# Scaling the values instead of the keys, and a last output tile in two halves, in a linear-attention and gated-MLP kernel

## The chip, the cores and the metric

The kernel runs on one core of one Trainium2 chip. The metric is the device time of one execution in microseconds (us), as a median over several runs. The core has five engines that work side by side and meet only at semaphores: TensorE (matmuls, PE in the profile), VectorE (DVE), ScalarE (ACT), GpSimd (POOL) and SyncE (SP, which here only starts transfers). TensorE writes to PSUM, eight banks of 512 fp32 columns; VectorE and ScalarE read PSUM[...].

## The reference

A token row of 2048 x 512 is layer-normalized, and two branches of it are added to the input: a linear attention with 32 heads of 16, and a gated MLP.

```python
qkv = (x @ wqkv) ...                      # q, k, v: (B, H, S, 16)
pq = einsum("bhsd,hdf->bhsf", q, w_phi)
pk = einsum("bhsd,hdf->bhsf", k, w_phi)
phi_q = concat([softmax(pq), softmax(-pq)])      # 32 features a head
phi_k = concat([softmax(pk), softmax(-pk)])
kv = einsum("bhsf,bhsd->bhfd", phi_k, v)
z  = einsum("bhsf->bhf", phi_k)
o  = einsum("bhqf,bhfd->bhqd", phi_q, kv) / (einsum("bhqf,bhf->bhq", phi_q, z) + 1e-6)
A  = o.reshape(B, S, D) @ wo
B  = (gelu(xn @ w_gate) * (xn @ w_up)) @ w_down  # 1376 wide
out = x + A + B                                  # xn = layernorm(x)
```

What matters for the change: a softmax over the 16 features of one head and one sign divides by a sum per token, head and sign. In the sum over tokens that makes `kv` and `z`, this divisor may be put on the key's exponentials or on the value and on a 1 beside it; the product is the same.

## The kernel before

The program lists its operations with what they read and write, and a small scheduler on the host puts them in an order for each engine; that order is fixed when the kernel runs. `BK` are the eight PSUM banks. The work goes by 16 tiles of 128 tokens. It starts with normalization, the first quarter of the MLP and the folding of `w_phi` into the key and query weights. Then comes the key/value stage (some 31 to 80 us of the span), and then attention output, the rest of the MLP and the output products, interleaved.

Start, with TensorE's spare matmuls, whose results nobody reads:

```python
op("pe", [... e.matmul(bank(7), warm[:, 0:128], warm[:]) for _ in range(11)], ...)
for t in range(4):
    ln_stats(t, ...); ln_rstd(t, 1); ln_norm(t)
    xt_pe(t, 4 + t % 2)            # 4 transposes on TensorE, copied to xnT by ScalarE
    if t < 2:
        op("pe", [... e.matmul(bank(3), warm[:, 0:128], warm[:]) for _ in range(2)], ...)
for t in range(4):
    gate4(t)                       # 16 matmuls of 128 columns
```

Key/value stage, by tile:

```python
def proj_k(t, b):                  # bank b from a ring of 4, shared with proj_q
    # 4 matmuls of 512 columns, then on ScalarE exp(+s) and exp(-s):
    e.activation(Ek[:, t, :, sig, :], bank(b)..., ACTF.Exp, scale=(1.0, -1.0)[sig])
    if t in SDVE:                  # (3, 7, 11, 15): one tensor_reduce on VectorE
        ...
    # the other 12 tiles: four halving additions on GpSimd, 512, 256, 128, 64 elements
    op("pool", ... e.tensor_tensor(o, a[:, :, 0:n], a[:, :, n:2 * n], op=ALU.add), ...)

def k_norm(t):                     # VectorE
    op("dve", ... e.reciprocal(rk[:, k, :], Ssum[:, t, :]), ...)
    op("dve", ... e.tensor_tensor(ev, ev, r, op=ALU.mult), ...)       # 1024 bf16, in place

def v_out(t, b):                   # copies V out of PSUM, ScalarE or VectorE
    alt([("act", ... ACTF.Copy), ("dve", ... tensor_copy)], ...)

def kv_acc(t):                     # banks 6 and 7, summed over all tiles
    for i in range(8):             # 4 heads x both signs on one side, 4 x 16 values and a 1
        e.matmul(ps[:, 3072 + i * 128:3072 + i * 128 + VB], Ek[:, t, i, :, :], vs[:, k, i, :], ...)
                                   # VB = 65 columns
def kv_finish():                   # 8 masked copies of 64 partitions into kvr
    ...
```

The output product of a tile, and what ends the kernel for the last four:

```python
def outp(t, b, direct):
    # 4 matmuls with wo and 11 with w_down, 512 columns each, into bank b
    if direct:
        op("dve", ... e.tensor_tensor(ob[:, k, :], bank(b), x_all[:, t, :], op=ALU.add), ...)
    ...
    dma("sp", ... e.dma_start(out2[t * P:(t + 1) * P, :], ob[:, k, :]), ...)
while outs < NT:
    outp(outs, (7, 0, 1, 2)[outs - 12], True)
```

Of the kernel before, what the change touches and what calls it, by code (L numbers as in the profile page):

```python
# [9 lines left out]
P = 128  # L10
# [10 lines left out]
VB = 4 * DH + 1  # L21
# [178 lines left out]
def bass_parallel_sum__linear_kernel_hedgehog__glu_gated_geglu__prompt_kernel(  # L200
# [14 lines left out]
    with ExitStack() as es, nc.allow_low_precision("bf16 softmax factors"):  # L215
# [13 lines left out]
        mask4 = sb([P, 4], f32, "mask4")  # L229
        hmask = sb([P, 8], f32, "hmask")  # L230
# [28 lines left out]
        NVS = 8  # L259
        vs = sb([P, NVS, 8, VB], bf16, "vs")  # L260
        NRK = 2
        rk = sb([P, NRK, 64], bf16, "rk")

# [15 lines left out]
        with nc.sbuf_tensor("Ek", [P, NT, 8, 2, 64], bf16) as Ek:  # L279
            pass  # L280
# [53 lines left out]
        B_rk = bufs("rk", NRK)  # L334
        B_vs = bufs("vs", NVS)
        B_m4, B_hm, B_v1 = Buf("m4"), Buf("hm"), Buf("v1")
        B_Eq = [bufs(f"Eq{s}_", 8) for s in range(NST)]
        B_wqT = B_Eq[3][0:4]
        B_kvr = bufs("kvr", 8)
# [105 lines left out]
        def proj_k(t, b):  # L445
            op("pe", [lambda e, i=i: e.matmul(  # L446
                bank(b), xnT[:, i, t * P:(t + 1) * P], wk2[:, i, :], start=(i == 0), stop=(i == 3))
                for i in range(4)], reads=[B_xnT[t]] + B_wk2, writes=[BK[b]], cost=mm(4))
            for sig in range(2):
                exps.append(op("act", lambda e, sig=sig: e.activation(  # L450
                    Ek[:, t, :, sig, :], bank(b).rearrange("p (b c) -> p b c", c=64), ACTF.Exp, scale=(1.0, -1.0)[sig]),
                    reads=[BK[b]], writes=[B_Ek[t][sig]], cost=0.55, extra=gelus, tab="exp"))
            ev = Ek[:, t, :, :, :].rearrange("p b s c -> p (b s) c")
            if t in SDVE:
                op("dve", lambda e: e.tensor_reduce(
                    Ssum[:, t, :].rearrange("p (g h) -> p g h", h=4), ev.rearrange("p g (f h) -> p g h f", h=4),
                    axis=mybir.AxisListType.X, op=ALU.add), reads=B_Ek[t], writes=[B_S[t]], cost=1.24)
                return
            v1 = st1[:].rearrange("p (g c) -> p g c", c=32)
            v2 = st2[:].rearrange("p (g c) -> p g c", c=16)  # L460
            v3 = st3[:].rearrange("p (g c) -> p g c", c=8)
            v4 = Ssum[:, t, :].rearrange("p (g c) -> p g c", c=4)
            for k, (o, a, n, bo, ba, c) in enumerate((
                    (v1, ev, 32, [B_st[0]], B_Ek[t], 1.17), (v2, v1, 16, [B_st[1]], [B_st[0]], 0.73),
                    (v3, v2, 8, [B_st[2]], [B_st[1]], 0.4), (v4, v3, 4, [B_S[t]], [B_st[2]], 0.29))):
                op("pool", lambda e, o=o, a=a, n=n: e.tensor_tensor(o, a[:, :, 0:n], a[:, :, n:2 * n], op=ALU.add),  # L466
                   reads=ba, writes=bo, cost=c, lock=k < 3)

        def k_norm(t):
            k = t % NRK  # L470
            op("dve", lambda e: e.reciprocal(rk[:, k, :], Ssum[:, t, :]), reads=[B_S[t]], writes=[B_rk[k]], cost=0.57)
            ev = Ek[:, t, :, :, :].rearrange("p b s (f h) -> p (b s) f h", h=4)
            r = rk[:, k, :].rearrange("p (g h) -> p g h", h=4).unsqueeze(2).to_broadcast([P, 16, DH, 4])
            op("dve", lambda e: e.tensor_tensor(ev, ev, r, op=ALU.mult), reads=[B_rk[k]], writes=B_Ek[t], cost=0.72,  # L474
               lock=True)
# [17 lines left out]
        def v_out(t, b):  # L493
            k = t % NVS
            dst, src = vs[:, k, :, 0:64], bank(b).rearrange("p (b c) -> p b c", c=64)
            alt([("act", lambda e: e.activation(dst, src, ACTF.Copy), 0.58),
                 ("dve", lambda e: e.tensor_copy(dst, src), 0.69)], reads=[BK[b]], writes=[B_vs[k]])

        SDVE = (3, 7, 11, 15)
        kv_first = [True, True]  # L500

        def kv_acc(t):
            k = t % NVS
            fns = []
            for i in range(8):
                st = kv_first[i // 4]
                kv_first[i // 4] = False
                fns.append(lambda e, i=i, st=st: e.matmul(  # L508
                    ps[:, 3072 + i * 128:3072 + i * 128 + VB], Ek[:, t, i, :, :], vs[:, k, i, :],
                    start=st, stop=(t == NT - 1), skip_group_check=True))  # L510
            op("pe", fns, reads=B_Ek[t] + [B_vs[k], B_v1], writes=BK[6:8], cost=8 * 0.045)

        def kv_finish():

            kv = ps[:, 3072:4096].rearrange("p (i c) -> p i c", c=128)
            for sg in range(2):
                for b2 in range(2):
                    src = kv[sg * 64:sg * 64 + 64, b2::2, :]
                    dst = kvr[b2 * 64:b2 * 64 + 64, sg * 4:sg * 4 + 4, b2 * 4:b2 * 4 + 4, :]
                    m = mask4[sg * 64:sg * 64 + 64, :].unsqueeze(1)  # L520
                    op("dve", lambda e, src=src, dst=dst, m=m: e.tensor_tensor(
                        dst[:, :, :, 0:DH], src[:, :, 0:64].rearrange("p i (h d) -> p i h d", d=DH),
                        m.unsqueeze(3).to_broadcast([64, 4, 4, DH]), op=ALU.mult),
                       reads=BK[6:8] + [B_m4, B_kvrm], writes=[B_kvr[sg * 4 + b2 * 2]], cost=dve(256))
                    op("dve", lambda e, src=src, dst=dst, m=m: e.tensor_tensor(
                        dst[:, :, :, DH], src[:, :, 64].unsqueeze(2).to_broadcast([64, 4, 4]),
                        m.to_broadcast([64, 4, 4]), op=ALU.mult),
                       reads=BK[6:8] + [B_m4, B_kvrm], writes=[B_kvr[sg * 4 + b2 * 2 + 1]], cost=0.2)
# [45 lines left out]
        def att(t):  # L574
            s, tl = t // 4, t % 4
            k = t % NB
            for q in range(3):
# [5 lines left out]
                   reads=B_Eq[s][3 * q:min(3 * q + 3, 8)] + B_kvr + [B_kvrm], writes=[BK[4 + q]],  # L583
# [61 lines left out]

        def wtrans(w, Bw, jj, b):
# [18 lines left out]
        NVG = 0  # L665
# [3 lines left out]
        for t in range(4):  # L669
# [4 lines left out]
            if t < 2:  # L674
                op("pe", [lambda e: e.matmul(bank(3), warm[:, 0:128], warm[:], start=True, stop=True)  # L675
                          for _ in range(2)], reads=[B_warm], writes=[BK[3]], cost=0.5,
                   extra=[d_tr[t]])
# [4 lines left out]
        def kq():  # L682
            turn[0] += 1
            return (turn[0] - 1) % 4
# [23 lines left out]
        for b2 in range(2):  # L708
            op("pool", lambda e, b2=b2: e.tensor_tensor(
                bd[:, :, b2 * 64:b2 * 64 + 64].rearrange("p j (f h) -> p j f h", h=4),  # L710
                mask8[:, b2 * 4:b2 * 4 + 4].unsqueeze(1).unsqueeze(1).to_broadcast([P, 4, DH, 4]),
                wphi[:].unsqueeze(3).to_broadcast([P, 4, DH, 4]),
                op=ALU.mult), reads=[B_mask8, B_wphi], writes=[B_bd], cost=0.6, lock=True,
                extra=[B_xn[3].last_write])
        op("dve", lambda e: e.tensor_reduce(
            mask4[:], idt_f[:].rearrange("p (a h) -> p h a", h=4), axis=mybir.AxisListType.X, op=ALU.add),
            reads=[B_idf], writes=[B_m4], cost=0.3)
        op("pool", [lambda e: e.memset(kvr[:].rearrange("p i h c -> p (i h c)"), 0.0),
                    lambda e: e.memset(hmask[:], 0.0)], writes=[B_kvrm, B_hm], cost=1.2)
        op("pool", lambda e: e.memset(vs[:, :, :, 64], 1.0), writes=[B_v1], cost=0.3)  # L720
        op("dve", [lambda e, b2=b2: e.tensor_copy(
            hmask[b2 * 64:b2 * 64 + 64, b2 * 4:b2 * 4 + 4], mask4[b2 * 64:b2 * 64 + 64, :]) for b2 in range(2)],
            reads=[B_m4], writes=[B_hm], cost=0.2)
        op("dve", lambda e: e.tensor_copy(
            kvr[:, :, :, VW], hmask[:].unsqueeze(1).to_broadcast([P, 8, 8])),
            reads=[B_hm], writes=[B_kvrm], cost=0.2)
# [6 lines left out]
        for jf in range(4, NF):  # L733
# [9 lines left out]
            if jf >= 6 and jf - 6 < NVG:  # L743
                proj_v(jf - 6, 4 + jf % 2)
                v_out(jf - 6, 4 + jf % 2)
# [10 lines left out]
        nk = 0  # L756

        def val(t):
            b = 4 + t % 2
            proj_v(t, b)  # L760
            v_out(t, b)

        def key():
            nonlocal nk
            k_norm(nk)
            if nk > 0:
                kv_acc(nk - 1)
            nk += 1
# [3 lines left out]
        for r in range(NT):  # L772
# [3 lines left out]
            if r + KA >= LAG:  # L776
                if NVG <= nk < NT:
                    val(nk)
                if nk < NT:
                    key()  # L780
        while nk < NT:
            if nk >= NVG:
                val(nk)
            key()
# [17 lines left out]
        while outs < NT:  # L802
            outp(outs, (7, 0, 1, 2)[outs - 12], True)
            outs += 1

# [52 lines left out]
```

## Time and profile before

| | |
|---|---|
| device time, median of 3 (lowest, highest) | 198.93 us (198.83, 199.02) |
| span of the profiled execution | 197.2 us |
| DMA | 14.41 MB, 73 GB/s on average |
| longest group of GpSimd's waits | 51.6 us, 16 times, for VectorE's `otmp` |
| longest group of ScalarE's waits | 42.1 us, 12 times, for the output products |
| final store: 16 of 128 KB, from issue to landing | 1.7 us (median) |

The profile is one execution on the chip. It has the busy time of each engine, the span in forty slices with a digit for the busy tenths, groups of instructions by source line with busy time and mean duration, waits with what ended them, and the chain of work that ended last: from the last instruction back, at each step to what released it or to the instruction before it on its engine. An engine with much idle time costs nothing as long as it doesn't keep that chain waiting. A row's mean duration of matmuls includes their overlap; what one adds to TensorE's list is read from the chain.

### The profile page before, as it was taken

How to read it: one execution, taken by the hardware profiler on the slowest of the kernel's cores; microseconds unless marked ns; L12 is line 12 of the kernel's file. 1: busy time of each engine (PE TensorE's matmuls, PEld its weight loads, DVE VectorE, ACT ScalarE, POOL GpSimd, SP SyncE). 2: the span in 40 equal slices, each digit the busy share in tenths (PEclk: the TensorE clock that was granted, in tenths of full speed). 3: DMA queues.
4: the chain of work that ended last, by engine and by line, in shares of the span. 5: the costliest groups of instructions: out<-in, count | busy, mean ns of one | idle time of the engine just before them, and what ended most of it. 6: DMA issues, size and time to landing. Idle time of an engine off the chain costs nothing.

```text
span 197.2 us, 3160 instructions
## 1 busy us (share of the span) xinstructions
PE 192.7 (98%) x1183; PEld 97.9 (50%) x1183; DVE 133.3 (68%) x312; ACT 86.2 (44%) x149; POOL 83.5 (42%) x109
## 2 busy tenths in 40 slices
PE   7999999999999999999999999999999999999994
PEld 2574665445545454554445555554545555454441
DVE  4789895469597767898695797948358494853121
ACT  2382798998887979323122132222223222221000
POOL 7731202799999996022244334242232324223100
PEclk9999999999999999999999999999999999999999
DMA  5999944456000000001221202120201111021101
GB/s 172 329 376 349 203 85 53 81 177 216 4 0 0 3 0 0 0 3 27 53 55 30 51 30 52 50 33 27 53 17 39 27 51 31 27 57 27 53 27 55
DMA packets 24079, 14.41 MB, mean 73 GB/s; under 512 B 15888, under 2 KB 23584, under 8 KB 24064
## 3 DMA queue, kind: packets, MB, share of 16 engines
q1 hardware_dynamic: 22944, 11.74, 23.4%
q0 software_dynamic: 560, 1.95, 3.1%
q10 hardware_dynamic: 560, 0.52, 0.8%
q8 instruction: 9, 0.15, 0.3%
q14 instruction: 6, 0.05, 0.1%
HBM read 8.44 MB, written 2.10 MB: 53 GB/s over the span
## 4 chain that ended last, share of the span: by engine, by line
PE 94%; DVE 2%; DMA 1%; POOL 1%; issue 0%
PE ps_all L546 35%; PE ps_all L630 18%; PE ps_all L489 7%; PE ps_all L478 7%; PE ps_all L446 7%; PE ps_all L626 7%; PE ps_all L578 4%; PE ps_all L667 2%; PE ps_all L508 2%; PE ps_all L561 2%; DMA oT<-o_sb 1%; PE ps_all L647 1%; PE ps_all L658 1%; PE ps_all L438 1%; PE ps_all L675 1%; POOL o_sb L618 1%
## 5 line engine op out<-in xcount | busy, mean ns | idle before, releaser
L546 PE MATMUL ps_all<-xnT,wu_sb 128*128 128x512 bf16 (+1 forms) x176 | 44.7, 379 | 0.0
L537 ACT ACTIVATE gs<-ps_all 128x512 bf16<-128x512 f32 (+1 forms) x44 | 25.9, 598 | 38.2 <-PE ps_all L546 38.1
L546 PE MATMUL ps_all<-xnT,wg_sb 128*128 128x512 bf16 (+1 forms) x160 | 40.9, 379 | 0.0
L630 PE MATMUL ps_all<-wd_sb,hT 128*128 128x512 bf16 (+1 forms) x176 | 40.6, 379 | 0.0
L618 POOL TENSOR_TENSOR o_sb<-otmp 128x512 bf16<-128x512 bf16 x16 | 18.5, 1154 | 51.6 <-DVE otmp L612 51.6
L539 DVE TENSOR_TENSOR hT<-gs,ps_all 128x512 bf16<-128x512 bf16 (+1 forms) x44 | 28.9, 680 | 14.7 <-PE ps_all L546 14.2
L630 PEld LDWEIGHTS ps_all<-wd_sb,hT 128*128 128x128 bf16 (+1 forms) x176 | 17.2, 98 | 20.8
L546 PEld LDWEIGHTS ps_all<-xnT,wu_sb 128*128 128x128 bf16 (+1 forms) x176 | 17.4, 100 | 19.4
L640 ACT ACTIVATE y_sb<-ps_all 128x512 f32<-128x512 f32 x12 | 7.2, 597 | 42.1 <-PE ps_all L630 42.1
L642 POOL TENSOR_TENSOR ob<-y_sb,x_all 128x512 bf16<-128x512 f32 x12 | 13.9, 1155 | 22.0 <-ACT y_sb L640 22.0
L612 DVE TENSOR_TENSOR otmp<-ps_all,cf 128x384 bf16<-128x384 f32 (+1 forms) x48 | 21.7, 507 | 0.6
L546 PEld LDWEIGHTS ps_all<-xnT,wg_sb 128*128 128x128 bf16 (+1 forms) x160 | 15.1, 100 | 13.7
L466 POOL TENSOR_TENSOR st<-st 128x256 f32<-128x256 f32 (+1 forms) x24 | 19.1, 795 | 1.8
L450 ACT ACTIVATE Ek<-ps_all 128x512 bf16<-128x512 f32 x32 | 17.3, 619 | 3.3 <-PE ps_all L446 2.9
L484 ACT ACTIVATE EqT<-ps_all 128x512 bf16<-128x512 f32 x32 | 17.8, 626 | 2.0 <-PE ps_all L478 1.7
L595 DVE RECIPROCAL r_sb<-ps_all 128x48 f32<-128x48 f32 (+1 forms) x32 | 9.2, 327 | 12.9 <-PE ps_all L578 12.8
L626 PE MATMUL ps_all<-wo_sb,oT 128*128 128x512 bf16 x64 | 16.4, 379 | 0.2 <-DMA oT<-o_sb 0.2
L489 PE MATMUL ps_all<-wv_sb,xnT 128*128 128x512 bf16 x64 | 16.4, 379 | 0.0
L478 PE MATMUL ps_all<-xnT,wq 128*128 128x512 bf16 x64 | 16.4, 379 | 0.0
L446 PE MATMUL ps_all<-wk,xnT 128*128 128x512 bf16 x64 | 15.9, 379 | 0.0
L466 POOL TENSOR_TENSOR st<-Ek 128x512 f32<-128x512 bf16 x12 | 13.9, 1157 | 3.7 <-ACT Ek L450 3.7
L474 DVE TENSOR_TENSOR Ek<-Ek,rk 128x1024 bf16<-128x1024 bf16 x16 | 14.6, 910 | 0.6
(71 smaller groups left out, 191.0 us busy)
## 6 DMA issues: line engine op xcount, KB each, us to landing
out_dram<-ob SPq DMA_DIRECT2D x16, 128.0 KB, 1.7
x_all<-in_A_x_dram SPq DMA_DIRECT2D x3, 512.0 KB, 9.3
wd_sb<-in_B_w_down_dram POOLq DMA_DIRECT2D x1, 1280.0 KB, 9.4
wg_sb<-in_B_w_gate_dram SPq DMA_DIRECT2D x2, 432.0 KB, 7.0
wu_sb<-in_B_w_up_dram SPq DMA_DIRECT2D x2, 432.0 KB, 8.1
wu_sb<-in_B_w_up_dram SPq DMA_DIRECT2D x2, 256.0 KB, 4.9
hT<-in_A_wqkv_dram SPq DMA_DIRECT2D x2, 256.0 KB, 8.0
EqT<-in_A_wqkv_dram SPq DMA_DIRECT2D x2, 256.0 KB, 9.1
```

Of the source, the lines that this page charges most:

```text
L446: op("pe", [lambda e, i=i: e.matmul(bank(b), xnT[:, i, t * P:(t + 1) * P], wk2[:, i, :], start=(i == 0), stop=(i == 3)) for i in range(4)] ...
L466: op("pool", lambda e, o=o, a=a, n=n: e.tensor_tensor(o, a[:, :, 0:n], a[:, :, n:2 * n], op=ALU.add), reads=ba, writes=bo, cost=c, lock=k < 3)
L478: op("pe", [lambda e, i=i: e.matmul(bank(b), wq2[:, i, p * 128:(p + 1) * 128], xnT[:, i, s * 512:(s + 1) * 512], start=(i == 0), stop=(i = ...
L484: exps.append(op("act", lambda e, g=g, sig=sig: e.activation(EqT[:, g, s * 512:(s + 1) * 512], bank(b), ACTF.Exp, scale=(1.0, -1.0)[sig]), ...
L489: op("pe", [lambda e, i=i: e.matmul(bank(b), xnT[:, i, t * P:(t + 1) * P], wv_sb[:, i, :], start=(i == 0), stop=(i == 3)) for i in range(4 ...
L537: h = op("act", lambda e: e.activation(gs[0:w, k, :], bank(gb)[0:w, :], ACTF.Gelu_apprx_tanh), reads=[BK[gb]], writes=[B_gs[k]], cost=0.55 ...
L539: op("dve", lambda e: e.tensor_tensor(hT[0:w, s % 2, jf, :], gs[0:w, k, :], bank(ub)[0:w, :], op=ALU.mult), reads=[B_gs[k], BK[ub]], write ...
L546: op("pe", [lambda e, i=i: e.matmul(bank(b)[0:w, :], wt[:, i, jf * 128:jf * 128 + w], xnT[:, i, s * 512:(s + 1) * 512], start=(i == 0), st ...
L612: op("dve", lambda e, q=q, n=n: e.tensor_tensor(otmp[:, k, q * 384:q * 384 + n * 128].rearrange("p (s h d) -> p s h d", s=n, d=DH), bank(4 ...
L618: op("pool", lambda e: e.tensor_tensor(o_sb[:, k, :], otmp[:, k, 0:512], otmp[:, k, 512:1024], op=ALU.add), reads=B_ot[k], writes=[B_o[k]] ...
L626: fns = [lambda e, j=j: e.matmul(bank(b), oT[:, t % NOT, j, :], wo_sb[:, j, :], start=(j == 0), stop=False) for j in range(4)]
L630: fns.append(lambda e, jf=jf, w=w: e.matmul(bank(b), hT[0:w, s % 2, jf, tl * 128:(tl + 1) * 128], wd_sb[0:w, jf, :], start=False, stop=(jf ...
```

## The change

Two things are asked of it. The normalization is moved from the exponentials of the keys to the values: the reciprocals are written beside the values as a 17th column of each head, and V is multiplied by them on its way out of PSUM. That does away with the in-place multiply of 1024 key elements and with a separate copy of V. The exponentials are kept in head order, with eight heads of one sign to a stationary tile, so each product has 8 x 17 = 136 columns, of which the blocks on the diagonal are used. The sums take three banks, so keys and queries share three in turn and values use banks 3 and 4. And the last output tile is computed in two halves of 256 columns in two banks, so that the first half's addition and store run under the second half's matmuls. The pair of spare matmuls behind the second tile's transposes goes.

```diff
-VB = 4 * DH + 1
+GV = 8 * VW                       # VW = 17
...
-        NVS = 8
-        vs = sb([P, NVS, 8, VB], bf16, "vs")
+        NVS = 5
+        vs = sb([P, NVS, 2, 4 * GV], bf16, "vs")
...
-                    Ek[:, t, :, sig, :], bank(b).rearrange("p (b c) -> p b c", c=64), ACTF.Exp, ...
+                    Ek[:, t, sig, :], bank(b), ACTF.Exp, ...
...
+            v1 = st1[:].rearrange("p (h f) -> p h f", f=8)
+            op("pool", lambda e: e.tensor_tensor(v1, ev[:, :, 0:8], ev[:, :, 8:16], op=ALU.add), ...
+            # then 4 + 4, 2 + 2 and 1 + 1 of each head
...
-        def k_norm(t): ...
-        def v_out(t, b): ...
+        def v_post(t, b):
+            op("dve", lambda e: e.reciprocal(
+                v[:, :, :, DH], Ssum[:, t, :].rearrange("p (s h) -> p s h", s=2)), ...
+            op("dve", lambda e: e.tensor_tensor(
+                v[:, :, :, 0:DH],
+                bank(b).rearrange("p (h d) -> p h d", d=DH).unsqueeze(1).to_broadcast([P, 2, 32, DH]),
+                v[:, :, :, DH].unsqueeze(3).to_broadcast([P, 2, 32, DH]), op=ALU.mult), ...
...
-                    ps[:, 3072 + i * 128:3072 + i * 128 + VB], Ek[:, t, i, :, :], vs[:, k, i, :],
+                    bank(5 + i // 3)[:, (i % 3) * GV:(i % 3 + 1) * GV],
+                    Ek[:, t, sig, p * 128:(p + 1) * 128],
+                    vs[:, k, sig, p * GV:(p + 1) * GV],
...
         def kv_finish():
-            # 8 masked copies, 64 partitions each
+            for q in range(3):     # 3 masked copies, one a bank
...
-            if t < 2:
+            if t < 1:
                 op("pe", [lambda e: e.matmul(bank(3), warm[:, 0:128], warm[:], ...) for _ in range(2)], ...
...
-            return (turn[0] - 1) % 4
+            return (turn[0] - 1) % 3
...
-            b = 4 + t % 2
+            b = 3 + nv % 2
...
-        while outs < NT:
-            outp(outs, (7, 0, 1, 2)[outs - 12], True)
+        while outs < NT - 1:
+            outp(outs, (7, 0, 1)[outs - 12], True)
             outs += 1
+        outp_halves(NT - 1, (2, 3))
```

The program's order of values, keys and products on TensorE's list changes with it: in the new one two tiles of values follow the first three of keys, and from the third tile on each tile's key-value products stand behind its own value product or the next one's.

## The prediction

> **What bounds the kernel now.** I read the page first (busy times and the forty slices), then TensorE's waits, then the chain of work that ended last in order of time, and last the rows and the timelines of the stage that the change rewrites.
>
> The page and the answer on TensorE's waits (us in total, times, longest):
>
> ```profile
> PE 192.7 (98%) x1183; PEld 97.9 (50%) x1183; DVE 133.3 (68%) x312; ACT 86.2 (44%) x149; POOL 83.5 (42%) x109
> ...
> PE   7999999999999999999999999999999999999994
> ...
> PE ps_all L667 <- DVE warm L393: 1.2, 1, 1.2
> PE ps_all L626 <- DMA oT<-o_sb: 0.2, 1, 0.2
> ```
>
> TensorE is busy in every slice but the first and the last, and after its first instruction it waits once, for 0.2 us. A busy row alone would not prove a bound, since matmuls overlap in it, so the proof is the chain (start, length, what):
>
> ```profile
> 7.85 0.22 PE ps_all L438 x4
> 8.07 0.43 PE ps_all L675 x2
> 8.51 0.67 PE ps_all L561 x12
> ...
> 40.05 0.26 PE ps_all L508 x8
> 40.31 0.86 PE ps_all L478 x4
> ...
> 83.90 0.50 PE ps_all L578 x8
> ...
> 191.87 2.39 PE ps_all L630 x11
> 194.26 0.02 issue
> 194.28 0.69 DVE ob L636
> ```
>
> The chain is 94% TensorE and its pieces join end to start. So whatever lengthens TensorE's list lengthens the kernel, and what the other engines save is worth nothing unless they come late. The chain also gives clean costs per matmul, which the mean of 379 ns in the rows does not (it contains the overlap): 0.86/4 = 216 ns at 512 columns, 0.50/8 = 62.5 ns at 144, 0.67/12 = 55.8 ns at 128, 0.26/8 = 32.5 ns at 65.
>
> The rows of VectorE that the change touches or that have a like form (busy us, mean ns):
>
> ```profile
> L612 DVE TENSOR_TENSOR otmp<-ps_all,cf 128x384 bf16<-128x384 f32 x32 | 16.4, 552 | 0.6
> L474 DVE TENSOR_TENSOR Ek<-Ek,rk 128x1024 bf16<-128x1024 bf16 x16 | 14.6, 910 | 0.6
> L612 DVE TENSOR_TENSOR otmp<-ps_all,cf 128x256 bf16<-128x256 f32 x16 | 6.6, 415 | 0.0
> ```
>
> GpSimd's timeline at the start of the same stage, tiles 0 to 2:
>
> ```profile
> 34.79 1.16 POOL L466 TENSOR_TENSOR st<-Ek 128x512 f32<-128x512 bf16 x1 [3.69 <-ACT Ek L450]
> ...
> 37.38 0.32 POOL L466 TENSOR_TENSOR Ssum<-st 128x64 f32<-128x64 f32 x1
> ...
> 44.66 1.60 POOL L466 TENSOR_TENSOR st<-st 128x256 f32<-128x256 f32 x2
> ```
>
> Tile 0's sums run from the first line shown to the second and tile 1's start at 37.66, so one tile takes GpSimd 2.87 us when left alone (its two middle sums 1.27). The last line is tile 2's middle pair, 1.60. In between stand three loads that GpSimd issues (39.40 to 41.78); they make the sums of tiles 1 and 2 the latest things in the stage.
>
> **What the Trainium skill says.** "TensorE: Matmul & The Clock Gate", section "Back-to-back issue gap": a warm matmul takes its columns over 2.4 GHz plus 2.5 ns. The trace agrees at 512, 144 and 128 columns; at 65 the formula gives 29.6 ns and the trace 32.5. The page's sustained figures with weight loads (81 ns at 128) don't hold here: 55.8 was measured with a load before each. "SBUF — State Buffer", section "Who interferes with whom": a VectorE instruction with two SBUF inputs shuts out a GpSimd instruction that reads SBUF, for its whole length. The trace agrees: the multiply of the keys takes 0.69 us alone and 1.04 otherwise, and GpSimd's pair of middle sums 1.27 us alone and 1.60 or 2.09 beside it. "VectorE: DVE Perf Modes", section "Why PSUM operands drop a tier": an fp32 operand in PSUM means the slowest mode. Row L612 agrees, at (552-415)/128 = 1.07 ns an element.
>
> **The change part by part.**
>
> *Key-value products.* Before, each of 16 tiles has 8 matmuls of 65 columns (four heads and a column of ones); after, 8 of 136 (eight heads, each with its reciprocal as a 17th column). The stationary side stays 128 wide, so nothing is won back. Between 55.8 ns at 128 and 62.5 at 144 lies 59.1 at 136: 0.473 us a tile against 0.26. 16 x 0.213 = **+3.4 us**, all on the chain.
>
> *Where the normalization sits.* Out go 16 multiplies of keys (910 ns) and the copies of V out of PSUM (9 on ScalarE of 0.61, 7 on VectorE of 0.69). In come 16 multiplies of 1024 elements out of PSUM: 552 + 640 x 1.07 = 1.24 us. VectorE pays 16 x 0.33 us more and saves 4.8: nearly even. ScalarE loses 5.5 us, GpSimd is no longer shut out. None of this lies on the chain: **0**, if nobody becomes late.
>
> *The spare matmuls.* The pair at 8.07 goes: 0.43 us. Behind it the 12 gate products of tile 0 are ready, and then come 4 of tile 1, whose copy by ScalarE ends at 8.71; TensorE would be there at 8.74. The later inputs (normalized tile 3 at 9.45, up weights issued at 3.5 to 4.4 and landing in about 5) are ready too: **-0.4 us**.
>
> *The last tile.* 30 matmuls of 256 columns, about 109 ns each, for 15 of 216: +0.03 us. The add behind the last matmul shrinks from 0.69 to about 0.42 us (the 415 of row L612 at 256 columns). The store is 64 KB where each one before is 128 KB and lands after 1.7 us, most of which I take for fixed; I allow 0.1. **-0.35 us.**
>
> *The one wait.* TensorE's 0.2 us before the third output tile: in the new order its attention products end 8.05 us before they are needed, against 7.55 before: **-0.2 us.**
>
> *New waits in the rewritten stage.* With 0.4 us gained, the first key products start at 31.0, exponentials at 33.2, GpSimd at 34.35. The sums of tile 1 are ready at about 43.0 (the three loads stand in between), its values at 44.85, TensorE reaches it at 45.3. The sums of tile 2 follow at 45.9, reciprocal and multiply by 47.7; TensorE is there at 47.5. So it waits about **+0.25 us**. Afterwards TensorE needs 3 x 0.86 + 0.47 = 3.06 us a tile, GpSimd 2.87 for three tiles of four, VectorE 0.55 for the reciprocal, 1.24, and a quarter of a 1.21 us sum, 2.1 in all, ScalarE four exponentials of about 0.5 = 2.0. All are faster than TensorE, so the lag does not come back.
>
> Sum: 3.4 - 0.4 - 0.35 - 0.2 + 0.25 = **+2.7 us**, and 198.93 + 2.7 = **201.6 us**, 1.4% more.
>
> **The rivals.**
>
> *The ring of score banks is too short.* Keys and queries get three PSUM banks in turn instead of four, values keep two, the sums take three. If ScalarE frees a bank only after TensorE wants it, TensorE waits at each group. For it: at the start ScalarE works off a backlog at 0.95 us a group against TensorE's 0.86. Against it: value and sum matmuls lie between; going through the first ten groups I find each bank free 0.5 to 1 us ahead. If it bites, about 0.2 us a tile: up to 3 us more, about 204.
>
> *VectorE or GpSimd becomes the bound.* If the new layout's short runs (8, 4, 2 and 1 elements) slow GpSimd's sums by a third, it needs 3.8 us a summed tile, 2.9 on average over four, still under 3.06, but the early wait grows to some 1 to 2 us: 202.5 to 203.5. Against it: three of its four steps read as many elements as before from tightly packed buffers.
>
> *The waits removed were worth more.* GpSimd freed from the lock and ScalarE from copies could only help if TensorE waited for them. Its waits above are 0.2 us in all, so I give this no weight. Were the wider matmuls hidden, the result would be 198.2; nothing in the chain speaks for hiding.
>
> **Range and chances.** The 3.4 us are the firm part, good to 0.2. The tail and the start may each miss by 0.2, the new waits lie between 0 and 2 us, so the range leans upwards: 200.8 to 203.0. 2% slower means 202.9, which takes one of the rivals: 0.13. Within 2%: 0.86. Faster by 2% would need 4 us from an engine that does not hold up the chain: 0.01.
>
> **What would show it.** The key-value row at 16 x 8 matmuls with about 0.47 us a tile in the chain, against 0.26; gate products straight behind the second tile's transposes; TensorE's waits a few tenths of a us, on VectorE at the third tile's sums; the last add near 0.42 us; GpSimd's middle sums at 1.27 us throughout. I am wrong if TensorE's list shows repeated waits on ScalarE (the ring) or on VectorE (late values), or if matmuls of 136 columns cost other than 59 ns.

## The result, and the profile after

| | before | after |
|---|---|---|
| device time, median of 4 runs each, side by side (lowest, highest) | 198.98 us (198.83, 199.62) | 201.30 us (200.82, 201.75) |
| ratio, 95% interval | | 1.011 [1.0076, 1.0144] |
| span of the profiled execution | 197.2 us | 199.1 us |

The changed kernel is 2.3 us slower, 1.1%. The prediction was 201.6 us, in a range of 200.8 to 203.0.

The page of the kernel after, busy times and the forty slices:

```profile
PE 195.0 (98%) x1196; PEld 102.6 (52%) x1196; DVE 130.9 (66%) x298; ACT 81.4 (41%) x140; POOL 75.6 (38%) x105
...
PE   7999999999999999999999999999999999999994
```

VectorE, ScalarE and GpSimd are less busy than before by 2.4, 4.8 and 7.9 us. TensorE is busier by 2.3 us. TensorE's waits after the change (us in total, times, longest) hold nothing from the rewritten stage:

```profile
PE ps_all L677 <- DVE warm L388: 1.2, 1, 1.2
PE ps_all L551 <- ACT xnT L437: 0.3, 1, 0.3
```

Both lie at the start. The 0.2 us for `oT<-o_sb`, the wait before the third output tile, is gone. The chain of work that ended last (start, length, what) is again TensorE's list, piece on piece:

```profile
6.91 0.38 PE ps_all L551 x4
7.29 0.22 PE ps_all L433 x4
7.51 0.67 PE ps_all L551 x12
8.18 0.02 issue
8.20 0.40 PE ps_all L551 x4
...
47.10 0.47 PE ps_all L503 x8
...
102.79 0.86 PE ps_all L616 x4
...
196.56 0.42 DVE ob L651
```

Set beside the chain before: the eight key-value products of a tile take 0.47 us where they took 0.26. The 12 gate products follow the second tile's transposes at once, but the next four take 0.40 us and not 0.22. The output tile at 102.79 starts with no gap. The last addition takes 0.42 us and not 0.69. VectorE's two new rows, as groups (busy us, mean ns, idle before and what ended it):

```profile
L487 DVE TENSOR_TENSOR vs<-ps_all,vs 128x1024 bf16<-128x1024 f32 x16 | 19.4, 1217 | 3.3 <-PE ps_all L477 3.2
L651 DVE TENSOR_TENSOR ob<-ps_all,x_all 128x256 bf16<-128x256 f32 x2 | 0.9, 426 | 2.2 <-PE ps_all L646 2.2
```

The multiply on the values takes 1.22 us, near the 1.24 worked out from a row of before. GpSimd's second sum of a tile, kept apart by shape:

```profile
L458 POOL TENSOR_TENSOR st<-st 128x256 f32<-128x256 f32 x12 | 8.8, 730 | 0.9
```

With the third, 400 ns in the same view, the middle pair takes 1.13 us in every tile, or 1.21 with the gap between the two, where 1.27 was predicted. Before, the two rows of these shapes were:

```profile
L466 POOL TENSOR_TENSOR st<-st 128x256 f32<-128x256 f32 x12 | 12.1, 1010 | 0.9
L466 POOL TENSOR_TENSOR st<-st 128x128 f32<-128x128 f32 x12 | 7.0, 580 | 0.9
```

With the pieces of the two chains the difference of the spans can be put together:

| part | from the chains | us |
|---|---|---|
| first gate product | 7.47 to 6.91 | -0.56 |
| spare pair: first gate product to first up product | 4.83 to 4.59 | -0.24 |
| key-value products, 16 tiles | 4.14 to 7.57 | +3.43 |
| wait before the third output tile | see experiments | -0.40 |
| matmuls of the last tile | 3.26 to 3.30 | +0.04 |
| end of the last matmul to the end | 2.94 to 2.57 | -0.37 |
| sum | spans: 197.2 to 199.1 | +1.90 |

Without the first row, which concerns matter ahead of everything changed, the sum is +2.46 us.

### The profile page after: what moved, and what is told of

The parts are those of the page before. It is cut to its first block, busy times and chain, and to the rows that moved or that the text cites. A ratio compares the mean times of both kernels' runs of the same rounds, so it can differ in the third digit from the quotient of the medians.

```text
span 199.1 us, 3159 instructions
## 1 busy us (share of the span) xinstructions
PE 195.0 (98%) x1196; PEld 102.6 (52%) x1196; DVE 130.9 (66%) x298; ACT 81.4 (41%) x140; POOL 75.6 (38%) x105
## 4 chain that ended last, share of the span: by engine, by line
PE 98%; DVE 0%; ACT 0%; issue 0%
PE ps_all L536 36%; PE ps_all L620 18%; PE ps_all L477 7%; PE ps_all L441 7%; PE ps_all L466 7%; PE ps_all L616 7%; PE ps_all L568 4%; PE ps_all L503 4%; PE ps_all L677 2%; PE ps_all L551 2%; PE ps_all L646 1%; PE ps_all L658 1%; PE ps_all L669 1%; PE ps_all L433 0%; PE ps_all L641 0%; ACT xnT L437 0%
## 5 line engine op out<-in xcount | busy, mean ns | idle before, releaser
L529 DVE TENSOR_TENSOR hT<-gs,ps_all 128x512 bf16<-128x512 bf16 (+1 forms) x44 | 28.7, 680 | 14.7 <-PE ps_all L536 14.6
L620 PE MATMUL ps_all<-wd_sb,hT 128*128 128x512 bf16 (+1 forms) x165 | 38.1, 379 | 0.0
L620 PEld LDWEIGHTS ps_all<-wd_sb,hT 128*128 128x128 bf16 (+1 forms) x165 | 16.1, 98 | 19.5
L487 DVE TENSOR_TENSOR vs<-ps_all,vs 128x1024 bf16<-128x1024 f32 x16 | 19.4, 1217 | 3.3 <-PE ps_all L477 3.2
L484 DVE RECIPROCAL vs<-Ssum 128x64 bf16<-128x64 f32 x16 | 8.7, 554 | 12.4 <-POOL Ssum L462 12.3
L616 PE MATMUL ps_all<-wo_sb,oT 128*128 128x512 bf16 x60 | 15.4, 379 | 0.0
```

The source lines that it names most:

```text
L487: op("dve", lambda e: e.tensor_tensor(v[:, :, :, 0:DH], bank(b).rearrange("p (h d) -> p h d", d=DH).unsqueeze(1).to_broadcast([P, 2, 32, DH]),
L529: op("dve", lambda e: e.tensor_tensor(hT[0:w, s % 2, jf, :], gs[0:w, k, :], bank(ub)[0:w, :], op=ALU.mult), reads=[B_gs[k], BK[ub]], write ...
L616: fns = [lambda e, j=j: e.matmul(bank(b), oT[:, t % NOT, j, :], wo_sb[:, j, :], start=(j == 0), stop=False) for j in range(4)]
L620: fns.append(lambda e, jf=jf, w=w: e.matmul(bank(b), hT[0:w, s % 2, jf, tl * 128:(tl + 1) * 128], wd_sb[0:w, jf, :], start=False, stop=(jf ...
```

## The experiments

Two theories were put against each other at the start. The one of the prediction: the extra columns of the key-value products are paid in full, because TensorE's list is the kernel; everything else is a few tenths. The rival: the size agrees by chance, and a good part of the loss comes from the ring of three banks, or from late values. The single parts were then measured one by one, most of them on the kernel before. A time "against before" is against runs of the kernel before on the same chip.

**One half of the change: the last tile in halves (e1_tail).** The kernel before, with the spare pair and normalized keys kept.

```diff
-        while outs < NT:
-            outp(outs, (7, 0, 1, 2)[outs - 12], True)
+        while outs < NT - 1:
+            outp(outs, (7, 0, 1)[outs - 12], True)
             outs += 1
+        outp_halves(NT - 1, (2, 3))
```

> The kernel before with only the last output tile in two halves. Theory (the tail is a serial chain behind the last matmul): matmuls of the last tile 3.30 us instead of 3.26, add behind the last matmul 0.43 instead of 0.69, end of the span 2.57 us after the last matmul instead of 2.94; in all 0.33 us less, 198.65. Rival (a store costs the same at any size): only the add shrinks, 0.22 us less. If the halves cost TensorE more than columns, the last tile takes over 3.4 us and nothing is gained.

Measured: 198.50 us (22 runs) against 198.86, ratio 0.9986 [0.9977, 0.9994], so -0.28 us by the ratio, with an interval of -0.46 to -0.12 (the medians differ by 0.36). The predicted -0.35 lies in it. Where it comes from is seen at the end of the kernel: the last addition 0.42 us in place of 0.69, and a store that lands earlier. The transfers at the end of the kernel after (KB each, median us from issue to landing):

```profile
out_dram<-ob SPq DMA_DIRECT2D x2, 64.0 KB, 1.5
```

In this view a store of half the bytes lands 0.2 us sooner after its issue than the 1.7 of the 128 KB stores. At the end of the span 0.1 us of that is left: the end follows the last matmul by 2.57 us and not 2.94, and 0.27 of these 0.37 us are the addition.

**One part: the second spare pair out (e2_nospare).** The kernel before with one edit:

```diff
-            if t < 2:
+            if t < 1:
                 op("pe", [lambda e: e.matmul(bank(3), warm[:, 0:128], warm[:], start=True, stop=True)
```

> The kernel before with only the second spare pair of matmuls taken out. Theory now: of its 0.43 us, 0.18 covered the wait for ScalarE's copy of the second tile, which then shows up in front of that tile's first gate products (0.40 us for the first four instead of 0.22); gain 0.24 us, 198.75. Rival (the prediction): gain 0.40. From the first gate product to the first 512-column product of the up weights: 4.83 us before, 4.59 by the theory, 4.43 by the rival.

Measured: 198.74 us (14 runs) against 198.86, ratio 0.9996 [0.9984, 1.0007], that is -0.32 to +0.14 us. The predicted -0.4 is outside, the -0.24 expected here inside; the time alone does not tell -0.24 from nothing. The chain does. With the pair (e1_tail):

```profile
8.13 0.22 PE ps_all L438 x4
8.36 0.43 PE ps_all L696 x2
8.79 0.67 PE ps_all L561 x12
9.46 0.22 PE ps_all L438 x4
```

Without it (e2_nospare):

```profile
8.26 0.22 PE ps_all L438 x4
8.49 0.67 PE ps_all L561 x12
...
9.18 0.40 PE ps_all L561 x4
9.57 0.22 PE ps_all L438 x4
```

From one group of transposes (L438) to the next there are 1.33 us with the pair and 1.31 us without. Removing 0.43 us of spare work wins nothing in that stretch, since the gate products of the second tile are now at the head of TensorE's list before ScalarE's copy is there. What is won comes later: those four products are then done, where with the pair they are among the 36 gate products that end the row (2.01 us; without it 32, 1.79 us). From the first gate product to the end of the last of them it is 4.84 us with the pair (7.75 to 12.59) and 4.60 without (7.88 to 12.48): -0.24 us, as in the changed kernel.

**The other half alone: the values scaled (e3_values).** The changed kernel with the old last tile and both spare pairs.

```diff
-            if t < 1:
+            if t < 2:
...
-        while outs < NT - 1:
-            outp(outs, (7, 0, 1)[outs - 12], True)
+        while outs < NT:
+            outp(outs, (7, 0, 1, 2)[outs - 12], True)
             outs += 1
-        outp_halves(NT - 1, (2, 3))
```

> The changed kernel with the old last tile and the spare pair back, so the move from keys to values alone. Theory (columns on TensorE's list): 16 x (0.473 - 0.26) = 3.4 us more, and about 0.4 less for the wait before the third output tile that the new order avoids: 3.0 us above before, 202.0. Rival (late engines, ring of three banks): TensorE's list of waits would show waits on ScalarE or VectorE between 31 and 84 us, and the sum would lie above 203.

Measured: 201.84 us (4 runs) against 198.86, ratio 1.0146 [1.0126, 1.0166], +2.9 us. TensorE has no wait in the stage, and every piece of key-value products is 0.47 us. The three parts, -0.28, -0.08 and +2.9, add up to +2.5 us; the whole change measured +2.3.

**The suspected cost taken away: products of 65 columns in the new form (e4_narrow).** The changed kernel, with its key-value products cut to the width they had before. This leaves out the products of about half of the heads.

```diff
-                    bank(5 + i // 3)[:, (i % 3) * GV:(i % 3 + 1) * GV],
+                    bank(5 + i // 3)[:, (i % 3) * GV:(i % 3) * GV + 65],
                     Ek[:, t, sig, p * 128:(p + 1) * 128],
-                    vs[:, k, sig, p * GV:(p + 1) * GV],
+                    vs[:, k, sig, p * GV:p * GV + 65],
```

> The changed kernel with its key-value products cut from 136 to 65 columns; it leaves out the products of the columns beyond, so half of the heads' sums are missing, and keeps everything else with the same order on TensorE. Theory (the columns are the whole price): 0.26 us a tile again, 3.4 us less than the changed kernel, 197.9, which is below before. Rival (layout, banks or VectorE cost something too): it stays above 199.5, with waits of TensorE in the stage.

Measured: 198.37 us (20 runs) against 198.86, ratio 0.9971 [0.9962, 0.9981]. So 201.3 falls to 198.4: 2.9 of the 3.4 us come back with the columns alone, ring, order, banks and engines being those of the change. From the first gate product to the end of the last matmul it takes 186.59 us (7.81 to 194.40), where the changed kernel has 189.62: 3.03 us less. A tile's products that wait for nothing take 0.24 us (0.26 in the kernel before), others more; the rest of the 3.43 us, 0.40, has become new waits, and with them the 197.9 us expected here were missed by 0.5. Two pieces of the chain, the first behind a wait, and TensorE's weight loads, which show on whom it waits (us in total, times, longest):

```profile
62.28 0.42 PE ps_all L503 x8
...
65.28 0.24 PE ps_all L503 x8
...
PEld ps_all L503 <- DVE vs L487: 2.2, 5, 0.6
```

With narrow products TensorE needs 2.82 us a tile (3 x 0.86 + 0.24), the kernel after's GpSimd 2.78 (36.77 - 33.99, between two tiles' first sums), and the values come late behind GpSimd's loads and behind tiles that VectorE sums. With wide products TensorE has 3.05 and the values are early. The new form would thus not have got the whole of its gain even with products as cheap as before.

**One size: three banks in turn (e5_ring3).** The kernel before, with the ring of keys and queries shortened.

```diff
-            return (turn[0] - 1) % 4
+            return (turn[0] - 1) % 3
```

> The kernel before with keys and queries in a ring of three PSUM banks instead of four, and nothing else. Theory (the ring is long enough, since value and sum products lie between): within 0.3 us of before, and no wait of TensorE on ScalarE in the key/value stage. Rival (the ring costs part of the 2.3 us of the change): 0.5 to 3 us slower, with waits of the key and query products on ScalarE's exponentials.

Measured: 199.19 us (13 runs) against 198.94, ratio 1.0013 [1.0004, 1.0022], +0.26 us. There is no wait on ScalarE in the key/value stage. TensorE's one wait behind the start, at the third output tile (`oT<-o_sb`), has grown from 0.24 to 0.38 us. That accounts for 0.14 of the 0.26 us. TensorE's timeline around it (start, length from the first start to the last end, and in brackets the idle time before it):

```profile
96.35 1.03 PE L626 MATMUL ps_all<-wo_sb,oT 128*128 128x512 bf16 x4
...
101.82 1.03 PE L546 MATMUL ps_all<-xnT,wg_sb 128*96 128x512 bf16 x4
103.22 1.04 PE L626 MATMUL ps_all<-wo_sb,oT 128*128 128x512 bf16 x4 [0.38 <-DMA oT<-o_sb]
```

From start to start the last two lines stand 1.40 us apart, where four matmuls that wait for nothing need 0.86. So this wait costs 0.54 us, 0.16 more than the list says. The first rival is small even where it shows, and what shows is another wait than it named.

**Is VectorE's and GpSimd's work worth anything? (e6_nomul)** The kernel before, with the keys' multiply cut to one feature in 16. This leaves out the normalization of the other 15; TensorE's list is the same.

```diff
-            op("dve", lambda e: e.tensor_tensor(ev, ev, r, op=ALU.mult), ...
+            op("dve", lambda e: e.tensor_tensor(ev[:, :, 0:1, :], ev[:, :, 0:1, :], r[:, :, 0:1, :], op=ALU.mult), ...
```

> The kernel before with the multiply of the keys cut from 16 features to one; it leaves out the normalization of the other 15, and TensorE's order is unchanged. Theory (what VectorE and GpSimd save does not lie on the chain): within 0.3 us of before, although VectorE saves about 13 us and GpSimd's middle sums fall from 1010 and 580 ns to 730 and 400. Rival (GpSimd freed from VectorE's lock shortens the kernel): 0.5 us or more below before.

Measured: 198.81 us (13 runs) against 198.94, ratio 0.9995 [0.9987, 1.0004]: no difference. A group of e6_nomul:

```profile
L466 POOL TENSOR_TENSOR st<-st 128x256 f32<-128x256 f32 x12 | 8.8, 733 | 0.9
```

Two things follow. VectorE loses 9.1 us of work (14.6 to 5.5; about 13 were expected) and GpSimd 4.8 us in its two middle sums (19.1 to 14.3; the 128-wide one now takes 454 ns) with no effect on the time, so savings on these engines lie off the path. And the sums in the old layout reach 733 ns as soon as the long multiply with two SBUF inputs is gone, from a mean of 1010. So it was the multiply that slowed them, and not the layout. That agrees with the Trainium skill, "SBUF — State Buffer", section "Who interferes with whom": a VectorE instruction with two SBUF inputs contends with a GpSimd instruction that reads SBUF, over a pair of ports that they share under an exclusive lock.

**The gains without the loss (e7_best).** Keys normalized as before, the last tile in halves, one spare pair, and the output products of the third tile placed later in TensorE's list (104.82 us in place of 102.98), so that the attention output is there. The last comes from a longer estimate for one transfer in the scheduler on the host, which changes only the order of work:

```diff
             dma("sp", lambda e: e.dma_start_transpose(oT[:, t % NOT, :, :], o_sb[:, k, :]),
-                reads=[B_o[k]], writes=[B_oT[t % NOT]], cost=1.2, lat=1.4, kb=310)
+                reads=[B_o[k]], writes=[B_oT[t % NOT]], cost=1.2, lat=2.2, kb=310)
...
-            if t < 2:
+            if t < 1:
...
+        outp_halves(NT - 1, (2, 3))
```

> The kernel before, keys scaled as there, with the three things that the traces show to help: last tile in two halves, no second spare pair, and an order on TensorE in which the third tile's attention output is asked for 8.5 us after its products instead of 7.2 (the scheduler is told 2.2 us for that transfer instead of 1.4). Theory: 0.33 + 0.24 + 0.40 = 0.97 us less than before, 197.9. Rival (the third wait only moves to another tile): 0.57 less, 198.3, with a wait on the attention output still in TensorE's list.

Measured: 197.91 us (5 runs) against 198.94, ratio 0.9955 [0.9942, 0.9967], -0.9 us by the ratio where -0.97 was expected. TensorE no longer waits for `oT`. From the first gate product (7.72) to the end of the last matmul (193.90) there are 186.18 us where the kernel before has 186.79: -0.61, of which -0.24 is the pair, +0.04 the narrower matmuls, and -0.41 the wait. That wait was listed at 0.2 us. In the kernel before, the chain at that place reads:

```profile
102.93 0.05 issue
102.98 1.04 PE ps_all L626 x4
```

In this view the four matmuls behind the wait take 1.04 us, where the same four take 0.86 in the kernel after (at 102.79). They are not slower: a piece of the chain that joins the one before counts from that one's end, and a piece behind a wait from its own start, as in the timeline of e5_ring3, where four such matmuls span 1.03 us without a wait. What is lost is the overlap with the matmuls ahead, and so a wait of 0.24 us costs 0.41.

**The change once more (e8_after).** The changed kernel as it is, to see how far its early start (6.91 us) is its own.

> The changed kernel once more, beside before on one chip. Theory: the parts read from the first pair of traces are 3.43 for the wider products, 0.24 less for the spare pair, 0.40 less for the avoided wait, 0.33 less for the last tile: 2.46 us above before, ratio 1.0124. The profile pair showed only 1.9 because the first gate product started 0.56 us earlier in it, which the theory takes for chance at the start: here the start should differ by less than 0.3 from the other runs of this call. Rival (the change itself starts earlier): the first gate product again about 0.5 us ahead of the kernels with the old start.

Measured: 201.28 us (4 runs) against 198.94, ratio 1.0113 [1.0097, 1.013], +2.3 us, as the first time. The first gate product is at 7.18 us in this execution, 0.35 to 0.54 ahead of the three other profiles of this chip (7.53, 7.56 and 7.72). The theory that it would lie within 0.3 of them failed; the rival, a start that comes earlier through the change, is not excluded. And the wait that the prediction spoke of is there, in the chain:

```profile
45.24 0.30 POOL Ssum L462
...
45.56 0.58 DVE vs L484
...
46.16 1.24 DVE vs L487
47.40 0.05 issue
47.45 0.65 PE ps_all L503 x8
```

The chain goes from GpSimd's sums to the reciprocal (L484), the multiply (L487) and then the products of the third tile, which take 0.65 us in place of 0.47. From the first gate product to the end of the last matmul there are 189.87 us here and 189.62 in the first profile: +0.25. GpSimd's timeline of the same execution says why the sums are later:

```profile
38.78 0.85 POOL L708 DMA_DIRECT2D wo_sb<-in_A_wo_dram  x1 [0.59 <-DMA xnT<-xn_sb]
```

GpSimd's three loads stand inside the sums of the second tile, behind the first of its four additions, and the first load waits 0.59 us for a transfer of the activations. In the first profile it did not wait, and counted from the first gate product the third tile's values came some 0.6 us earlier.

**That wait by itself (e10_loads).** The changed kernel, with the three loads put behind the third tile's sums in GpSimd's list. TensorE's list is the same.

```diff
+        for h in self.late:
+            order.remove(h)
+        k = order.index(self.anchor) + 1
+        order[k:k] = self.late
         self._emit(order)
```

> The changed kernel with the three loads that GpSimd issues moved behind the sums of the third tile in its list; TensorE's order is unchanged. Theory (these loads make the third tile's values the latest thing of the stage, by the amount of their own wait for a transfer): the second and third tiles' sums are ready 2.4 us or more earlier, and TensorE never waits for values in the stage, so the chain from the first gate product to the last matmul is 189.6 us, as in the first profile of the changed kernel, and not 189.9, as in the second; time 201.2, hard to tell from 201.3. Rival (the late values come from VectorE's own queue): the wait of TensorE at the third tile's key-value products is still there.

Measured: 201.43 us (5 runs) against 198.92, ratio 1.0131 [1.0111, 1.0152]. GpSimd's timeline around the third tile's last sum:

```profile
42.81 0.29 POOL L466 TENSOR_TENSOR Ssum<-st 128x64 f32<-128x64 f32 x1
43.05 0.85 POOL L714 DMA_DIRECT2D wo_sb<-in_A_wo_dram  x1
```

The sums are ready at 43.10 us in place of 45.54, no product waits for values, and from the first gate product (7.65) to the end of the last matmul (197.28) there are 189.63 us, as in the first profile of the change without the wait. So the place of these loads, together with their wait, makes the values late; one profile each shows it. In time it can't be seen: 0.25 us is inside the intervals, and this execution began 0.47 us later than the one of e8_after.

**The last tile in 384 and 128 columns (e9_split).** The kernel of e7_best with another cut.

```diff
-            for h, b in enumerate(bs):
-                c = slice(h * 256, h * 256 + 256)
+            for h, b in enumerate(bs):
+                n = (384, 128)[h]
+                c = slice(h * 384, h * 384 + n)
```

> The best version so far (keys scaled, no second spare pair, later third attention output) with the last tile split in 384 and 128 columns instead of 256 and 256. Theory (the add and the bytes behind the last matmul count): the add falls from 0.42 to about 0.29 us (137 ns for 128 elements, as between the rows of 384 and 256), the last tile's matmuls stay at 3.3 us, the end follows the last matmul after about 2.4 us instead of 2.57: 0.15 to 0.2 us less, 197.75. Rival (runs of 256 bytes in the store cost more than the bytes save): nothing gained or a loss, the store landing later than 1.5 us.

Measured: 197.83 us (6 runs) against 198.92, ratio 0.9948 [0.9933, 0.9963]. The chain of e9_split ends:

```profile
192.63 0.63 PE ps_all L657 x11
...
193.29 0.29 DVE ob L662
```

The last addition is 0.29 us, and from the last matmul to the end there are 2.34 us in place of 2.57. That is 0.2 us in the trace, but against e7_best (197.91) the times don't tell it: the intervals overlap.

## Why the prediction was right

*Key-value products, +3.4 us.* Measured +3.43 in the chain. A tile costs 0.47 us, 59 ns a matmul of 136 columns. The formula for the gap of a single warm matmul in the Trainium skill, "TensorE: Matmul & The Clock Gate", section "Back-to-back issue gap", gives 136/2.4 + 2.5 = 59.2 ns; the trace agrees, although here a weight load stands ahead of each matmul, for which the page has other figures. Removing the columns alone gives 2.9 us back in time and 3.03 in the chain. That most of the loss is this one term is shown, and not only argued.

*Where the normalization sits, 0.* Right: e6_nomul takes 14 us of work from VectorE and GpSimd, and the time stays.

*The spare matmuls, -0.4.* Mis-sized; the term is -0.24. The prediction took a copy that ends at 8.71 as ready for TensorE's arrival at 8.74. But 8.74 is the end of the 12 products ahead, and in an unbroken list the next matmul starts 0.16 us before that end, at about 8.58. In the chain of the change the four gate products come 0.02 us behind the list and then take 0.40 us, 0.18 more than four that wait for nothing: 0.2 of the 0.43 us are a wait for the copy.

*The last tile, -0.35.* Right: +0.04 for the narrower matmuls, and -0.37 at the end, in sum -0.33. By the time of e1_tail -0.28.

*The one wait, -0.2.* Mis-sized, -0.40: the prediction took the idle time of the list, and the list leaves out the lost overlap, here 0.17 us.

*New waits, +0.25.* They come and go: none in the first profile or in that of e3_values, 0.25 us in the second of the change, at the tile, by the chain and of the size that the working gave. The sums of the third tile were expected at 45.9 and the values at 47.7; measured were 45.54 and 47.40.

The sum of these is +2.46 us without and +2.71 us with the late values, where +2.7 was predicted. The two mis-sized terms (0.16 too much won at the start, 0.2 too little at the third output tile) cancelled each other; that the total came so close is in part luck. The measured +2.3 us lies a little below both sums. +2.46 is inside the intervals of the first measurement and of e8_after (+1.9 to +2.6 us); +2.71 is above the latter. The earlier start may be the reason, see below.

*The rivals.* The ring of three banks makes no wait on ScalarE, in either form, and costs 0.26 us on the kernel before. GpSimd's sums did not suffer from the short runs of the new layout: 730 and 400 ns, against 733 and 454 in the old layout with nothing beside it. What was taken from VectorE and GpSimd was worth nothing; ScalarE's copies were not taken out alone, but in the profiles of the kernel before TensorE has no wait on ScalarE in the stage.

What stays open is the start. The first gate product comes at 6.91 and 7.18 us in the two profiles of the change, and at 7.08 to 7.88 in the five other kernels with a single pair (e2_nospare, e7_best, e9_split and, in the new form, e4_narrow and e10_loads); with both pairs at 7.47 to 7.76. It is ahead of everything that was changed, and the landing of the gate weights, which stands ahead of it in the chains of eight of the twelve profiles, varied from execution to execution. Whether the change has a share in its early starts was not settled.

## What to carry to other kernels

When one engine's list joins end to end, count columns: what the rewrite added to that engine was paid in full here, and 14 us saved on its neighbours were worth nothing. A block-diagonal product costs its whole width, though each head uses only 17 of the 136 columns, so moving a cheap elementwise step off other engines is not a reason to widen it. Of a change in several parts, build the parts singly: here three small gains (the last tile, the spare pair, the avoided wait) were hidden under the loss, and without it they make 197.9 us out of 198.9.

## What the runs showed of the hardware

A wait of TensorE cost some 0.17 us more than its listed idle time, at every width that was seen: 0.41 us for 0.24 listed ahead of matmuls of 512 columns, 0.25 for 0.07 at 136 columns (e8_after), 0.2 for 0.02 at 128. The matmuls behind the wait were not slower. A matmul's record lasts longer than the distance to the next start: 379 against 216 ns at 512 columns, 219 against 55.8 at 128, both 163 ns more. In an unbroken list each one thus starts 0.16 us before the end of the one ahead, while the idle time of a wait counts from that end. An estimate of what a wait costs is therefore its idle time plus 0.16 us. The ends of matmuls are modelled in the profile, but the starts alone say the same, as in e5_ring3: 0.54 us late for 0.38 listed.

The start of an execution varies by more than the parts that were measured here: the first gate product lay between 6.91 and 7.88 us in the profiles. A part of a few tenths is better read between two fixed events of the chain, as was done here from the first gate product to the last matmul, than from the spans.
